# A chunked recurrence with an FFN on one core: other streams of constants on TensorE ahead of chunks 0 and 1

## The chip, the cores and the metric

One core of one Trainium2 chip. The metric is the device time of one execution in microseconds (us), as the median over runs. A smaller number is better. The engines are named as in the profile: PE is TensorE (PEld its weight loads), DVE is VectorE, ACT is ScalarE, POOL is GpSimd, and SP is the engine that issues most of the DMAs.

## The reference

First a recurrence with a state per head (batch 4, 8 heads, 768 steps, head size 48), then a feed-forward network over its output (3072 tokens, 384 wide, 2048 hidden), all in float32:

```python
for t in range(S):
    kt, vt, rt, wt = (k[:, :, t], v[:, :, t], r[:, :, t], w[:, :, t])
    cur = np.einsum('bhd,bhe->bhde', u[None] * kt, vt)
    y[:, :, t] = np.einsum('bhd,bhde->bhe', rt, state + cur)
    state = wt[:, :, :, None] * state + np.einsum('bhd,bhe->bhde', kt, vt)
...
h = x @ w_in
g = h * (1.0 / (1.0 + np.exp(-1.702 * h)))
return (g @ w_out).astype(np.float32)
```

## The kernel before, in words

**Tiling.** The recurrence is cut into 24 chunks of 128 steps (6 for each batch, numbered t = 0 to 23). A chunk has all 8 heads in 4 pairs. For one chunk, `chunk(t)` does these steps, in this order, with a `yield` between them:

- two running products of the decay on DVE (L352, L357), and the scaled k and r, `kq`, on DVE (L363);
- four transposes of the scaled k on PE into `ps_t` (L373), copied to `kt` by ACT (L375);
- the product r*k, `rku`, on DVE (L384), and the diagonal products `ps_d` on PE (L396), copied to `s` by ACT (L399), from which ACT makes the diagonal blocks `am` (L406, 8 instructions);
- the state products (L427) and the products of k and r (L431) on PE into `ps_u`;
- the new state on DVE (L437 to L441; the first chunk of a batch copies on ACT, L435), and the masked blocks put into `am` on DVE (L444);
- the output products on PE into `ps_y`: those with `am` (L454), the first half of those with the state (L467, `inter(True)`), then a copy of one element by ACT into `mid` (L477), which the second half (`inter(False)`, L467 again) has to wait for, then the copy out (L491, or L279 and L280).

A third generator, `measures` (token m), has ACT square and sum a chunk's running products (L285). The feed-forward network is done in tasks of one block of 128 hidden units by up to 512 tokens: first product (g, L526 plain or L531 to L533 split), gelu (h) and second product (y, L566 or L569 to L571). Weights are fetched (f) and converted (w) on ACT and DVE (L261 to L275) in the first 100 us or so.

**What sets the order.** The program is scheduled by hand. The string `RAMP` is a list of tokens, each of which issues one step: `a3` is the next step of chunk 3, `l2` the next loads of chunk 2, `m1` the measure of chunk 1, `g0`, `h0`, `y0` the steps of task 0. Each engine runs its own instructions in the order in which they were issued. After RAMP, rules set the order.

**The streams of constants.** A token `d6` does not issue work by itself. It puts (6, 4) on the list `cold`; the next call of `bank`, which hands out a PSUM bank, takes it off and issues six matmuls of a constant tile `warm` (128x128 in bfloat16, all ones, set by DVE in L124) with itself, 512 columns each, into the bank that was just handed out (L313). What they write is overwritten by the products that the bank was taken for.

```python
while cold:
    times, n = cold.pop()
    for _ in range(times):
        T.matmul(x.rearrange("p (n c) -> p n c", c=P)[:, 0:n], warm, warm_b[:, 0:n], start=True, stop=True)
```

In the kernel before, `d20` stands at the start (ahead of chunk 0's transposes), `d6` ahead of chunk 1's transposes, and after them `d5`, `d3`, `d7` and `d2` in other places. In the trace all of them have line L313.

Of the kernel before, what the change touches and what calls it, by code (L numbers as in the profile page):

```python
# [9 lines left out]
F32 = mybir.dt.float32  # L10
F32R = mybir.dt.float32r
BF16 = mybir.dt.bfloat16
# [10 lines left out]
P = 128  # L23
# [3 lines left out]
R2 = HB + D  # L27
# [55 lines left out]
AHEAD = (1, 1, 2, 2)  # L83
FIRST = 37
RAMP = """
d20 l0 l0 l1 a0 a0 a0 M m0 a0 a0 a1 a1 l0 a0 a0 a0 f0 a1 d6 l2 a0 a1 a1 a1 l1 l2 m1 a0 l3 a1 a1 a2 a2 a1 a1 a0 a0 d5
a2 w0 a3 a0 d3 a1 a2 d7 a1 a2 f1 a3 a3 a2 l3 a1 f2 x1 w1 a2 a2 a3 l4 a3 a3 a3 w0 a2 a2 d2 m2 f3 d2 a3 g0 w1 a3 h0 a3
a2 w2 w2 g1 h1 a2 y0 a2 a3 a4 w3 l4 g2 f4 a3 w3 h2 a3 w1 a4 w0 y1 w2 g3 y2 w0 h3 g4 w3 h4 m3 a4 w2 w4 y3 y4 f5 x3 s0
w1 a4 a4 g5 g6 w4 h5 w3 s0 w5 g7 h6 f6 w5 l5 g8 y5 w4 h7 a4 l6 f7 w4 a4 l5 h8 a4 a5 g9 y6 f8 h9 a5 w5 g10 y7 w5 w6 y8
y9 a5 h10 g11 w7 m4 a5 w6 f9 y10 a4 a5 a4 w6 h11 w8 w7 w6 g12 w7 a4 w8 a5 y11 g13 w7 a5 f11 h12 g14 y12 a6 h13 f10 a6  # L90
w9 y13 w9 l7 h14 w8 a5 w11 w8 a5 a4 m5 g15 a6 y14 w10 a5 a7 w9 a6 w10 g16 a6 h15 w9 h16 w11 g17 l8 w10 a6 a6 w10 y15
w11 w11 y16 g18 h17 a4 l6 a7 h18 u a5 a6 a5 l7 a7 m6 a6 a6 a8 g19 a7 a7 a5 a8 h19 y17 a6 m7 a7 a7 l8 a6 a7 a7 a8 a7 a6
l9 y18 a8 a8 a8 a9 l10 a7 l9 a8 a8 a7 a7 g20 a9 y19 x7 h20 a9 a8 a8 m8 y20 l10 a10 g21 a9 a9 h21 a10 l11 g22 a9 y21
h22 a9 a8 a9 a8 a9 m9 a9 a10 a11 y22 g23 a10 a10 a10 g24 a8 h23 a9 l11 a10 a11 a10 a9 a11 h24 a10 y23 m10 a11 a11 y24
a11 a9 g25 a11 l12 a10 a11 a11 a11 l13 h25 a10 a11 a10 a10 a12 a12 m11 a12 a11 a13 a11 a12 y25 l12 g26 l14 g27 g28 h26
g29 y26 g30 h27 g31 a13 y27 h28 a12 m12 h29 h30 g32 y28 g33 h31 a13 a13 y29 y30 y31 h32 g34 h33 h34 g35 y32 g36 h35
y33 h36 y34
"""
WIDE = 512
GAP = 64  # L100
# [8 lines left out]
def rwkv_ffn_kernel(ctx: ExitStack, tc, wkr, vp, vrk, ub, w_in, w_out, masks, vt, uc, out):  # L109
# [10 lines left out]
    at = fast.enter_context(tc.tile_pool(name="at", bufs=1))  # L120


    warm = at.tile([P, P], BF16, name="warm")
    V.memset(warm, 1.0)  # L124
    hm = cp.tile([R2, 2 + 2 * H], F32, name="hm")
    G.memset(hm, 0.0)
# [38 lines left out]


    A.activation(at.tile([R2, 1], F32, tag="s", name="junk", bufs=2), hm[:, 0:1], AF.Gelu_apprx_sigmoid)
    warm_b = warm.unsqueeze(1).broadcast_to([P, WIDE // P, P])

    his, los, whole = {}, {}, {}  # L170

# [133 lines left out]
    def bank(name):  # L305

        i = free.pop(0)
        x = ps_a.tile([P, WIDE], F32, tag=f"bank{i}", name=name)
        held[id(x)] = i, x
        while cold:  # L310
            times, n = cold.pop()
            for _ in range(times):
                T.matmul(x.rearrange("p (n c) -> p n c", c=P)[:, 0:n], warm, warm_b[:, 0:n], start=True, stop=True)  # L313
        return x

    def release(*xs):
# [290 lines left out]
    with tc.manual_schedule():  # L607
        early = ExitStack()
        su = early.enter_context(tc.tile_pool(name="su", bufs=1))
        where = [(i, col) for i, n in enumerate(CHUNKS) for col in range(n)]  # L610
        starts = [sum(CHUNKS[:i]) for i in range(len(CHUNKS))]
        last = {}
        for j, task in enumerate(TASKS):
            last[task[0]] = j
        running, told = {}, {}

        def piece(kind, i):

            if (kind, i) not in running:
                running[kind, i] = {  # L620
                    "l": load, "a": chunk, "m": measures.get, "w": lambda i: convert(i, su, False),
                    "s": lambda i: split_x(),
                }[kind](i)
            next(running[kind, i])

        def do(token):
            kind, i = token[0], int(token[1:] or 0)
            told[token] = told.get(token, 0) + 1
            if kind in "lamws":
                piece(kind, i)  # L630
                if kind == "w" and all(told.get(f"w{n}") == 4 for n in range(2 * NL)):
                    early.close()
                    pools["late"] = fast.enter_context(tc.tile_pool(name="late", bufs=2))

                    pools["late"].tile([P, GAP], F32, tag="gap", name="gap", bufs=1)
                    xs[1] = new_x(1)
            elif kind == "f":
                fetch(i, su)
            elif kind == "x":
                group, col = where[i]  # L640
                if i == 1:
                    fill_x(xw[0].unsqueeze(1) if WHOLES else xs[group], 0, 2 * C)
                elif i == 3:
                    fill_x(xs[group], 2 * C, 4 * C)
                elif group and col == CHUNKS[group] - 1:
                    fill_x(xs[group], 0, (col + 1) * C)
            elif kind in "de":
                cold.append((i, WIDE // P if kind == "d" else 2))
            elif kind == "u":
                pools["u"] = pools["late"].tile([P, DM], F32, tag="u", name="u_sb", bufs=1)  # L650
                nc.sync.dma_start(pools["u"], ub)
            elif kind == "M":
                nc.sync.dma_start(hm[ROWS, 0 : 2 + H], masks)
            elif kind == "g":
                first_product(i, TASKS[i])
            elif kind == "h":
                gelu(i, TASKS[i])
            elif kind == "y":
                group = TASKS[i][0]
                if i in (len(TASKS) - 9, len(TASKS) - 4):  # L660
                    next(judged)
                if i == len(TASKS) - 1:
                    bad.append(nc.values_load(cnt, min_val=0, max_val=full) < full)
                    finish(i)
                elif i < len(TASKS) - 3:
                    second_product(i, TASKS[i])
                if i == last[group] and i < len(TASKS) - 1:
                    store(group, starts[group] * C, CHUNKS[group] * C)

        def judge():  # L670

            sums = acc[:, NT : 3 * NT]
            V.tensor_tensor(sums, sums, sums, op=ALU.mult)
            for x, limit in ((acc[:, 0 : 3 * NT], LIMIT), (acc[:, 3 * NT :], W_MAX)):
                V.tensor_single_scalar(x, x, limit, op=ALU.is_lt)
            oks = at.tile([P, 1], F32, tag="s", name="oks", bufs=2)
            V.tensor_reduce(oks, acc, axis=AX.X, op=ALU.add)
            yield  # L680
            got = bank("ps_n")
            ps = got[0:1, 0:1]
            T.matmul(ps, oks, oks, start=True, stop=True)
            V.tensor_copy(cnt, ps)
            release(got)
            yield

        cnt = acc[0:1, 0:1].bitcast(I32)
        full = P * acc.shape[1] ** 2
        bad, judged = [], judge()  # L690

        def rest():

            begins = []
            for t, (i, col) in enumerate(where):
                n = len([x for x in TASKS if x[0] == i - 1])
                begins.append(last.get(i - 1, -1) + 1 - BEFORE - round((CHUNKS[i] - 1 - col) * n / CHUNKS[i]))
            left = []
            for t, begin in enumerate(begins):
                ramp = dict(told)  # L700
                for k, (kind, step, half, rank) in enumerate(PARTS):
                    token = f"{kind}{t + 2 * (kind == 'l')}"
                    if t in BY_BLOCKS and k < len(AHEAD):
                        step -= AHEAD[k] + (k == 3 and where[t][1] == 2)
                    elif t + 2 in BY_BLOCKS and kind == "l" and step == 3:
                        step -= 2
                    if kind == "l" and t + 2 >= NT:
                        continue
                    if ramp.get(token, 0):
                        ramp[token] -= 1  # L710
                    else:
                        left.append((step + begin, half, rank, token))
            left.sort(key=lambda x: x[:3])
            for j in range(FIRST, len(TASKS) + LAG):
                for post in range(3):
                    if post and j < len(TASKS):
                        yield f"{'gh'[post - 1]}{j}"
                    while left and left[0][:2] <= (j, post):
                        yield left.pop(0)[3]
                if j - LAG >= 0 and f"y{j - LAG}" not in told:  # L720
                    yield f"y{j - LAG}"

        for token in RAMP.split():
            do(token)
        for token in rest():
            do(token)
# [119 lines left out]
```

## Time and profile before

| | |
|---|---|
| median of 3 runs | 494.29 us (493.68 to 495.75) |
| the profiled execution | 494.09 us |
| its span, first to last instruction | 492.4 us |
| PE busy | 482.0 us (98%) |
| DVE busy | 298.9 us (61%) |
| ACT busy | 227.1 us (46%) |
| mean granted TensorE clock | 0.997 of full speed |
| DMA moved | 51.60 MB, mean 105 GB/s |

The profiled execution took 1.7 us more than its span, which lies around the first and the last instruction. A busy PE is not a PE at its peak: the end of a matmul is modelled, and a small matmul counts some 0.2 us from start to end however few columns it has. The granted clock is told as a share of full speed, where 1.00 is 2.4 GHz and 0.50 is 1.2 GHz.

### The profile page before, as it was taken

What the parts mean: (1) busy time and instruction counts of PE and PEld (TensorE: products, weight loads), DVE (VectorE), ACT (ScalarE), POOL (GpSimd) and SP (SyncE); (2) the same over time, 40 slices, a digit from 0 to 9 for tenths busy, and PEclk for the clock granted to TensorE, in tenths of its full rate; (3) what the DMA queues carried; (4) which work ended last, traced back from release to release, by engine and by line L of the source; (5) the groups of instructions that cost most, each with busy time, mean ns of one, the idle gap of its engine ahead of it and who ended that gap; (6) DMA issues with size and microseconds to landing.
All of it is one profiled execution on the core that took longest, in us unless ns stands there. A gap on an engine that the chain in (4) does not pass through costs nothing.

```text
span 492.4 us, 11658 instructions
## 1 busy us (share of the span) xinstructions
PE 482.0 (98%) x4891; PEld 395.0 (80%) x4891; DVE 298.9 (61%) x508; ACT 227.1 (46%) x518; POOL 15.9 (3%) x49
## 2 busy tenths in 40 slices
PE   7999999999999999999999999999999999999996
PEld 3678988887877887888888878888888878888885
DVE  8989999989888333855755745745845421111211
ACT  3799999865354332533433532342542332322221
POOL 3011000001001000000001000001000000000000
PEclk9899999999999999999999999999999999999999
DMA  8986949155721425062243252243340001100002
GB/s 220 260 242 193 276 128 237 48 148 157 208 57 34 124 88 117 23 185 81 81 119 98 75 173 71 81 140 85 92 154 20 4 1 32 64 1 0 1 0 73
DMA packets 34254, 51.60 MB, mean 105 GB/s; under 512 B 4336, under 2 KB 24240, under 8 KB 34192
## 3 DMA queue, kind: packets, MB, share of 16 engines
q1 hardware_dynamic: 33152, 48.84, 34.0%
q0 software_dynamic: 784, 1.39, 1.3%
q8 instruction: 40, 0.66, 0.6%
q10 hardware_dynamic: 256, 0.52, 0.3%
q14 instruction: 22, 0.18, 0.1%
HBM read 40.88 MB, written 7.60 MB: 98 GB/s over the span
## 4 chain that ended last, share of the span: by engine, by line
PE 84%; DVE 5%; DMA 4%; ACT 2%; issue 2%; SPq 1%; POOL 1%; DVEq 0%; ACTq 0%; POOLq 0%
PE ph L531 12%; PE po L569 12%; PE ph L533 11%; PE ph L532 11%; PE po L571 11%; PE po L570 11%; PE ps_y L467 3%; PE ps_y L454 2%; PE ps_u L431 2%; PE ps_u L427 2%; DMA far<-kb 2%; DMA kx<-far 2%; PE ph L526 1%; PE po L566 1%; PE po L595 1%
## 5 line engine op out<-in xcount | busy, mean ns | idle before, releaser
L551 DVE TENSOR_TENSOR gl<-gf,gh 128x512 fp32r<-128x512 f32 (+1 forms) x96 | 64.6, 673 | 145.5 <-ACT gf L549 144.8
L548 ACT ACTIVATE gh<-ph 128x512 fp32r<-128x512 f32 (+1 forms) x96 | 56.3, 586 | 185.5 <-PE ph L533 173.2
L531 PE MATMUL ph<-x,h 128*128 128x512 f32 (+1 forms) x288 | 111.5, 387 | 0.1
L533 PE MATMUL ph<-x,l 128*128 128x512 f32 (+1 forms) x288 | 110.6, 384 | 0.0
L532 PE MATMUL ph<-x,h 128*128 128x512 f32 (+1 forms) x288 | 110.5, 384 | 0.0
L569 PE MATMUL po<-gh,h 128*128 128x512 f32 (+1 forms) x279 | 109.5, 392 | 0.0
L571 PE MATMUL po<-gl,h 128*128 128x512 f32 (+1 forms) x279 | 107.3, 385 | 0.0
L570 PE MATMUL po<-gh,l 128*128 128x512 f32 (+1 forms) x279 | 107.2, 384 | 0.0
L531 PEld LDWEIGHTS ph<-x,h 128*128 128x128 f32 x288 | 54.1, 188 | 11.2 <-DMA x<-x 0.5
L533 PEld LDWEIGHTS ph<-x,l 128*128 128x128 f32 x288 | 54.1, 188 | 10.8
L532 PEld LDWEIGHTS ph<-x,h 128*128 128x128 f32 x288 | 54.2, 188 | 10.4
L571 PEld LDWEIGHTS po<-gl,h 128*128 128x128 f32 x279 | 52.5, 188 | 10.9 <-DVE gl L551 0.4
L569 PEld LDWEIGHTS po<-gh,h 128*128 128x128 f32 x279 | 52.4, 188 | 10.7
L570 PEld LDWEIGHTS po<-gh,l 128*128 128x128 f32 x279 | 52.5, 188 | 9.7
L549 ACT ACTIVATE gf<-ph 128x512 f32<-128x512 f32 (+1 forms) x96 | 56.0, 583 | 4.7 <-DVE gl L551 4.6
L363 DVE TENSOR_TENSOR kq<-wkr_t,lp 112x1024 f32<-112x1024 f32 x24 | 29.3, 1222 | 1.1 <-PE ps_y L467 0.6
L352 DVE TENSOR_TENSOR_SCAN lp<-wkr_t,d1r 112x516 f32<-112x516 f32 x24 | 29.4, 1224 | 0.9 <-POOL same L154 0.9
L357 DVE TENSOR_TENSOR_SCAN lp<-wkr_t,d1f 112x516 f32<-112x516 f32 x24 | 29.4, 1225 | 0.1
L285 ACT ACTIVATE junk<-lp 112x1032 bf16<-112x1032 f32 x24 | 25.5, 1065 | 5.2 <-DVE lp L357 5.2
L467 PE MATMUL ps_y<-kq,mid 48*48 48x64 f32 (+3 forms) x384 | 23.1, 218 | 1.4 <-ACT mid L477 1.1
L510 POOL DMA_DIRECT2D x<-x x18 | 9.0, 507 | 371.1 <-DVE x L280 199.0
L467 PEld LDWEIGHTS ps_y<-kq,mid 48*48 48x48 f32 (+3 forms) x384 | 18.7, 127 | 2.7 <-ACT mid L477 1.2
(107 smaller groups left out, 511.9 us busy)
## 6 DMA issues: line engine op xcount, KB each, us to landing
st<-in_w_out SPq DMA_DIRECT2D x6, 1024.0 KB
rk_t<-in_vrk SPq DMA_DIRECT2D x16, 384.0 KB
st<-in_w_in SPq DMA_DIRECT2D x6, 896.0 KB
v_t<-in_vrk SPq DMA_DIRECT2D x24, 192.0 KB
out_t<-ob SPq DMA_DIRECT2D x15, 256.0 KB
wkr_t<-in_wkr SPq DMA_DIRECT2D x18, 192.0 KB
wkr_t<-in_wkr SPq DMA_DIRECT2D x36, 96.0 KB
wkr_t<-in_wkr SPq DMA_DIRECT2D x5, 577.9 KB
```

The lines of the kernel that those rows point to most:

```text
L352: V.tensor_tensor_scan(li[:, ::-1], w1[:, ::-1], d1r.rearrange("r p c -> r (p c)")[:, ::-1], 0.0, op0=ALU.mult, op1=ALU.add)
L357: V.tensor_tensor_scan(pm, w0, d1f.rearrange("r p c -> r (p c)"), 0.0, op0=ALU.mult, op1=ALU.add)
L467: T.matmul(ps[b][head(h), p], from_[head(half), p * D + OFF * h : p * D + HB], qf[head(half), p, blocks[b]], start=False, stop=p == PAIRS[ ...
L531: T.matmul(ph, h_, xs[i][:, 0, c, cs], start=c == 0, stop=False)
L532: T.matmul(ph, h_, xs[i][:, 1, c, cs], start=False, stop=False)
L533: T.matmul(ph, l_, xs[i][:, 0, c, cs], start=False, stop=c == NM - 1)
L548: A.activation(gh, ph, AF.Gelu_apprx_sigmoid, scale=1.0 / W_SCALE)
L549: A.activation(gf, ph, AF.Gelu_apprx_sigmoid, scale=1.0 / W_SCALE)
L551: V.tensor_tensor(gl, gf, gh.bitcast(F32), op=ALU.subtract)
L569: T.matmul(o, h_, gh, start=first, stop=False, skip_group_check=True)
L570: T.matmul(o, l_, gh, start=False, stop=False, skip_group_check=True)
L571: T.matmul(o, h_, gl, start=False, stop=f == NF - 1, skip_group_check=True)
```

## The change

The constant tile becomes 128x112 in float32. A second view of it, `lights`, reads its first 64 columns as 128 columns of bfloat16 (so that ones and zeros alternate). The old tokens d use `lights`. A new token c issues float32 matmuls: 112x112 weights, 4 times 112 columns. The list `cold` is now emptied in the order in which it was filled. In RAMP, `d20` becomes `c5 d7`, `d6` becomes `d7`, and two tokens `d1` are new: one ahead of chunk 1's diagonal products and one ahead of its state products. A float32 matmul leaves two records in the trace (as the `ps_d` products do, 4 matmuls and 8 records), so that the 20 + 6 records of before stand against 10 + 7 + 7 + 1 + 1 = 26 records of the change.

```diff
 RAMP = """
-d20 l0 l0 l1 a0 a0 a0 M m0 a0 a0 a1 a1 l0 a0 a0 a0 f0 a1 d6 l2 a0 a1 a1 a1 l1 l2 m1 a0 l3 a1 a1 a2 a2 a1 a1 a0 a0 d5
...
+c5 d7 l0 l0 l1 a0 a0 a0 M m0 a0 a0 a1 a1 l0 a0 a0 a0 f0 a1 d7 l2 a0 a1 a1 d1 a1 l1 l2 m1 a0 l3 a1 d1 a1 a2 a2 a1 a1 a0
...
-    warm = at.tile([P, P], BF16, name="warm")
+    warm = at.tile([P, R2], F32, name="warm")
     V.memset(warm, 1.0)
...
-    warm_b = warm.unsqueeze(1).broadcast_to([P, WIDE // P, P])
+    lights = warm.bitcast(BF16)[:, 0:P]
+    warms = [x.unsqueeze(1).broadcast_to([P, WIDE // P, x.shape[1]]) for x in (warm, lights)]
...
         while cold:
             times, n = cold.pop()
             for _ in range(times):
-                T.matmul(x.rearrange("p (n c) -> p n c", c=P)[:, 0:n], warm, warm_b[:, 0:n], start=True, stop=True)
+                w = warms[n > 0]
+                m, k = w.shape[2], n or WIDE // P
+                T.matmul(x.rearrange("p (n c) -> p n c", c=P)[0:m, 0:k, 0:m], w[:, 0], w[:, 0:k], start=True, stop=True)
...
-            elif kind in "de":
-                cold.append((i, WIDE // P if kind == "d" else 2))
+            elif kind in "cde":
+                cold.insert(0, (i, {"c": 0, "d": WIDE // P, "e": 2}[kind]))
```

The rest of RAMP holds the same tokens in the same order. On DVE only the size of the constant's memset differs, and on ACT, POOL and SP nothing does.

**The first place** is the start of PE's order, up to chunk 0's transposes (`ps_t<-ident,kq`). Before, it ends with the last of twenty pairs of a weight load and a matmul:

```order
L313 LDWEIGHTS warm
L313 MATMUL ps_t<-warm 128x512
L373 MATMUL ps_t<-ident,kq_89 128x112 x4
L396 MATMUL ps_d<-hm,rku 128x2 x4
L427 MATMUL ps_u_194<-v_t_86,kt 64x48
```

With the change, where every line after the head of the file stands three lower (L316 for L313), five float32 matmuls and seven pairs stand there, of which the first is shown:

```order
L844 UNCONDITIONAL_BRANCH
L316 MATMUL ps_t<-warm 112x4x112 x5
L316 LDWEIGHTS warm
L316 MATMUL ps_t<-warm 128x512
...
L376 MATMUL ps_t<-ident,kq_89 128x112 x4
L399 MATMUL ps_d<-hm,rku 128x2 x4
```

Nothing else moved there: the transposes, the diagonal products and the state products of chunk 0 follow without a stream between them, as before.

**The second place** is chunk 1 on PE, from the last product of chunk 0's `ps_u` to chunk 1's first state product. Before (the first of six pairs is shown):

```order
L431 MATMUL ps_u_195<-kq_89 64x64
L313 LDWEIGHTS warm
L313 MATMUL ps_t<-warm 128x512
...
L373 MATMUL ps_t<-ident,kq_90 128x112 x4
L396 MATMUL ps_d<-hm,rku 128x2 x4
L427 MATMUL ps_u_274<-v_t_87,kt 64x48
```

With the change (the first of seven pairs is shown):

```order
L434 MATMUL ps_u_187<-kq_89 64x64
L316 LDWEIGHTS warm
L316 MATMUL ps_t<-warm 128x512
...
L376 MATMUL ps_t<-ident,kq_90 128x112 x4
L316 LDWEIGHTS warm
L316 MATMUL ps_d<-warm 128x512
L399 MATMUL ps_d<-hm,rku 128x2 x4
L316 LDWEIGHTS warm
L316 MATMUL ps_u_268<-warm 128x512
L430 MATMUL ps_u_268<-v_t_87,kt 64x48
```

One pair is added ahead of the transposes, one between them and the diagonal products, and one between these and the state products.

## Rows read from the trace of the kernel before

**Rows 1.** The page: busy time by engine; then PE's granted clock in 40 slices.

```profile
PE 482.0 (98%) x4891; PEld 395.0 (80%) x4891; DVE 298.9 (61%) x508; ACT 227.1 (46%) x518; POOL 15.9 (3%) x49
...
PEclk9899999999999999999999999999999999999999
```

**Rows 2.** Stretches: window, length, busy PE, PEld, DVE, ACT, POOL, granted clock, DMA.

```profile
7.52:9.29 1.77, 0.00 (x0) 0.03 (x1) 1.74 (x3) 1.16 (x2) 0.00 (x0) 1.00 1.03 271
9.29:11.82 2.53, 2.53 (x76) 2.35 (x76) 2.46 (x4) 1.37 (x5) 0.00 (x0) 1.00 1.04 223
11.82:15.24 3.42, 3.42 (x19) 1.78 (x12) 3.39 (x7) 1.55 (x7) 0.00 (x0) 0.50 0.86 244
15.24:19.79 4.55, 3.46 (x122) 3.23 (x121) 4.13 (x8) 4.36 (x14) 0.00 (x0) 1.00 0.84 225
```

**Rows 3.** The chain that ended last, 9 to 23 us: start, length, what.

```profile
9.16 0.14 issue
...
11.94 2.67 PE ps_t L313 x6
...
15.40 0.53 ACT kt L375
15.93 1.05 ACT junk L285 x2
16.98 0.06 ACT s L399
...
19.09 0.05 ACT mid L477
...
19.85 1.83 PE ps_y L313 x8
...
22.77 0.53 PE ps_t L373 x4
```

**Rows 4.** PE in order of time: start, length, what, count, [idle before].

```profile
1.14 6.38 PE L313 MATMUL ps_t<-warm 128*128 128x512 bf16 x20 [1.14 <-DVE warm L124]
9.29 0.57 PE L373 MATMUL ps_t<-ident,kq 112*128 112x112 f32 x4 [1.77 <-DVE kq L363]
...
14.41 0.95 PE L373 MATMUL ps_t<-ident,kq 112*128 112x112 f32 x4
...
19.18 0.67 PE L467 MATMUL ps_y<-kq,mid 64*64 64x64 f32 x8 [1.09 <-ACT mid L477]
```

**Rows 5.** A later stretch, columns as in rows 2.

```profile
20.00:25.00 5.00, 5.00 (x82) 3.10 (x81) 4.86 (x6) 3.75 (x14) 0.00 (x0) 1.00 1.03 292
```

**Rows 6.** Weight loads of the first stream in order of time.

```profile
4.53 0.15 PEld L313 LDWEIGHTS <-warm 128*128 128x128 bf16 x1 [0.28 <-issue]
4.96 2.06 PEld L313 LDWEIGHTS <-warm 128*128 128x128 bf16 x10 [0.28 <-issue]
```

**Rows 7.** The chain at 42 us: six records of float32 products, 256 columns.

```profile
42.83 1.29 PE po L566 x6
```

**Rows 8.** DVE in order of time, chunk 1's `kq` and what follows.

```profile
12.41 1.23 DVE L363 TENSOR_TENSOR kq<-wkr_t,lp 112x1024 f32<-112x1024 f32 x1
...
18.88 0.77 DVE L444 COPY_PREDICATED am<-after,ps_u 128x256 f32<-128x256 int32 x2
19.89 1.23 DVE L363 TENSOR_TENSOR kq<-wkr_t,lp 112x1024 f32<-112x1024 f32 x1 [0.24 <-PE ps_y L467]
...
26.35 0.69 DVE L384 TENSOR_TENSOR rku<-wkr_t 112x512 f32<-112x512 f32 x1 [0.82 <-PE ps_d L396]
```

**Rows 9.** ACT in order of time, chunk 0's diagonal products read.

```profile
10.89 0.17 ACT L399 COPY s<-ps_d 128x8 f32<-128x8 f32 x1 [0.46 <-PE ps_d L396]
```

**Rows 10.** In order of time: a weight fetch (SP), its first reader (ACT), row copies (POOL).

```profile
14.91 1.35 SPq L243 DMA_DIRECT2D st<-in_w_out  x1
...
24.69 1.14 ACT L261 ACTIVATE st<-st 128x1024 int32<-128x1024 uint32 x1
...
25.10 1.60 POOL L510 DMA_DIRECT2D l<-l  x3 [19.93 <-ACT l L491]
```

More of the change, by code (lines that the diff above doesn't have):

```diff
@@ L85 @@
 RAMP = """
-d20 l0 l0 l1 a0 a0 a0 M m0 a0 a0 a1 a1 l0 a0 a0 a0 f0 a1 d6 l2 a0 a1 a1 a1 l1 l2 m1 a0 l3 a1 a1 a2 a2 a1 a1 a0 a0 d5
[L87 to L95, printed above, removed]
@@ L96 @@
-g29 y26 g30 h27 g31 a13 y27 h28 a12 m12 h29 h30 g32 y28 g33 h31 a13 a13 y29 y30 y31 h32 g34 h33 h34 g35 y32 g36 h35
-y33 h36 y34
+c5 d7 l0 l0 l1 a0 a0 a0 M m0 a0 a0 a1 a1 l0 a0 a0 a0 f0 a1 d7 l2 a0 a1 a1 d1 a1 l1 l2 m1 a0 l3 a1 d1 a1 a2 a2 a1 a1 a0
+a0 d5 a2 w0 a3 a0 d3 a1 a2 d7 a1 a2 f1 a3 a3 a2 l3 a1 f2 x1 w1 a2 a2 a3 l4 a3 a3 a3 w0 a2 a2 d2 m2 f3 d2 a3 g0 w1 a3
+h0 a3 a2 w2 w2 g1 h1 a2 y0 a2 a3 a4 w3 l4 g2 f4 a3 w3 h2 a3 w1 a4 w0 y1 w2 g3 y2 w0 h3 g4 w3 h4 m3 a4 w2 w4 y3 y4 f5
+x3 s0 w1 a4 a4 g5 g6 w4 h5 w3 s0 w5 g7 h6 f6 w5 l5 g8 y5 w4 h7 a4 l6 f7 w4 a4 l5 h8 a4 a5 g9 y6 f8 h9 a5 w5 g10 y7 w5
@@ new lines @@
+w6 y8 y9 a5 h10 g11 w7 m4 a5 w6 f9 y10 a4 a5 a4 w6 h11 w8 w7 w6 g12 w7 a4 w8 a5 y11 g13 w7 a5 f11 h12 g14 y12 a6 h13
+f10 a6 w9 y13 w9 l7 h14 w8 a5 w11 w8 a5 a4 m5 g15 a6 y14 w10 a5 a7 w9 a6 w10 g16 a6 h15 w9 h16 w11 g17 l8 w10 a6 a6
+w10 y15 w11 w11 y16 g18 h17 a4 l6 a7 h18 u a5 a6 a5 l7 a7 m6 a6 a6 a8 g19 a7 a7 a5 a8 h19 y17 a6 m7 a7 a7 l8 a6 a7 a7
+a8 a7 a6 l9 y18 a8 a8 a8 a9 l10 a7 l9 a8 a8 a7 a7 g20 a9 y19 x7 h20 a9 a8 a8 m8 y20 l10 a10 g21 a9 a9 h21 a10 l11 g22
+a9 y21 h22 a9 a8 a9 a8 a9 m9 a9 a10 a11 y22 g23 a10 a10 a10 g24 a8 h23 a9 l11 a10 a11 a10 a9 a11 h24 a10 y23 m10 a11
@@ L98 @@
+a11 y24 a11 a9 g25 a11 l12 a10 a11 a11 a11 l13 h25 a10 a11 a10 a10 a12 a12 m11 a12 a11 a13 a11 a12 y25 l12 g26 l14 g27
+g28 h26 g29 y26 g30 h27 g31 a13 y27 h28 a12 m12 h29 h30 g32 y28 g33 h31 a13 a13 y29 y30 y31 h32 g34 h33 h34 g35 y32
+g36 h35 y33 h36 y34
 """
```

## The prediction

> **What bounds the kernel now.** I read the page first [rows 1]: PE is busy 98% of the span, and its granted clock is clearly below full in one slice alone, the second (12 to 25 us). So PE sets the time, and what the change can win or lose lies in the first 25 us. The busy time by stretches [rows 2] shows the place: PE idle from 7.52 to 9.29 us, small products until 11.82 at a granted 1.00, then 3.42 us at 0.50 (1.2 GHz), and 1.00 again (2.4 GHz) from 15.24 us.
>
> The chain of waits [rows 3] tells whether this costs time. It runs through the six constant matmuls ahead of chunk 1's transposes (2.67 us), through these transposes at the lower clock, then through ACT (the copy of `kt`, the measure L285, `s`, the eight `am`, the copy into `mid`), and back to PE at 19.18 us for the second half of chunk 0's output products. PE had waited 1.09 us for that copy [rows 4]. From 20 us on it has no idle time in the next stretch [rows 5]. So what chunk 1's transposes gain or lose comes out at 19.18 us, and moves a PE that hardly rests afterwards.
>
> **Durations.** In the first stream the weight loads, one for each matmul, are 0.43 us apart until 4.96 us (4.53 to 4.96), and then ten of them take 2.06 us, 0.21 apart [rows 6]. For 512 columns that is the pace of 1.2 GHz and then of 2.4 GHz, although the granted clock stands at 1.00 from the start. So in this execution the clock rose near 5.0 us, 3.8 us after the stream's start at 1.14 [rows 4]. The trace has no float32 matmul of 448 columns. The nearest row is six float32 records of 256 columns in 1.29 us, 0.215 each [rows 7]; by columns that makes 0.215 x 448/256 = 0.376 us for one record at full clock (estimate), and 0.75 at half.
>
> **The change part by part.**
>
> *`c5 d7` for `d20`.* Ten float32 records and seven bfloat16 ones stand against twenty. With the clock rising at 4.96 us as before, five records at 0.75 from 1.2 us end at 4.95, five at 0.376 end at 6.83, and seven at 0.215 end at 8.33 us. Before, the stream ended at 1.14 + 6.38 = 7.52. Chunk 0's transposes wait for DVE's `kq` and start at 9.29 either way [rows 4], so the direct cost is nothing, and PE's idle time ahead of them falls from 1.77 to 0.96 us. If the rise came one microsecond later, the end would move by about half of that (each record started at half clock costs 0.37 more, and one starts every 0.75); the cover is gone where the rise comes after some 6.6 us.
>
> *`d7` for `d6`, and the clock there.* This decides the sum. If the clock stays at full, seven matmuls take 7 x 0.215 = 1.5 us from 11.94, until 13.44. Then chunk 1's transposes wait for their `kq`, which DVE ends at 12.41 + 1.23 = 13.64 [rows 8]. With the 0.14 us that lay between the two for chunk 0 [rows 3] they start at 13.78, take chunk 0's 0.57 instead of 0.95 [rows 4], and end at 14.35. They ended at 14.41 + 0.95 = 15.36. That is 1.01 us.
>
> *The two `d1`.* 0.215 us each, on PE. From the end of chunk 1's transposes to the wait at 19.18 - 1.09 = 18.09, PE's products took 2.73 us; with both `d1` they end at 14.35 + 2.73 + 0.43 = 17.51. ACT, 1.01 earlier, reaches the `mid` copy at 18.08, so PE still waits for ACT, by half a microsecond. The diagonal products ended 0.99 us after chunk 0's transposes (ACT took them at 10.89, after a wait [rows 9]); with one `d1` that is 15.6 for chunk 1, and ACT wants them at 16.98 - 1.01 = 15.97. Both `d1` are covered; without that cover they would cost 0.43.
>
> *The memset, the order of `cold`, the bits of `lights`.* Nothing: the tile is 448 bytes per partition against 256, on a DVE that soon waits for POOL; only `c5` and `d7` are ever on the list together; and the columns are as many.
>
> *Does the microsecond live on?* The second half of chunk 0's output products starts at 18.17 instead of 19.18. DVE's next `kq` waited only 0.24 us for it [rows 8], because DVE is busy with `am` until 19.65. It comes 0.24 earlier, then, and ends at 20.88, while PE, 1.01 earlier, wants it for chunk 2's transposes at 21.76 (22.77 in [rows 3]): no wait. Further on DVE waits 0.82 us for PE's `ps_d` at 26.35 [rows 8], and there it gains what it lacked. Two things need not move with PE: the weight fetch issued at 14.91 and read at 24.69, and the copies of rows issued at 25.10 [rows 10]. The read shows no wait, and the copies are issued by what PE and ACT finish, so I let both move. If the fetch lands only just in time today, nothing of the gain is left: the lower end, 0. The upper end is 1.01, because DVE's `kq` forbids more. I take **0.95**, near the upper end, as no row shows a wait on that way.
>
> *Is the clock held?* Here I chose. Chunk 0: 4.42 us without a stream (7.52 to 11.94), of it 1.77 idle, and the clock fell at 11.82 [rows 2]. Chunk 1: from the end of its stream (11.94 + 2.67 = 14.61) to the next at 19.85 there are 5.24 us without one, of it 1.09 idle, and the clock stayed at 1.00 [rows 2 to 4]. The changed kernel has 3.6 us without a stream (8.33 to 11.94), of it 0.96 idle: less of both than the stretch that held. By the nearer row the clock holds.
>
> **Sum.** Against the profiled execution's own time: 494.09 - 0.95 = 493.1. The median of the runs stands 0.2 above that execution, so the forecast is **493.3 us**. That is 0.2%; about 0.5% (2.5 us) is what a measurement of this kernel can tell from no change.
>
> **The rivals.**
>
> *The clock falls all the same.* For it: chunk 0's own products from 9.29 to 11.82 are unchanged, and they are the last that PE does before the fall. Against it: the same kinds of product kept 1.00 after chunk 1's stream. Then `d7` is one matmul more at half clock, 0.43 us, ahead of the transposes; as these then lie further into the time after the rise at 15.24, they end 0.25 to 0.43 later, and the two `d1` stay under ACT. Result 494.3 + 0.35 = 494.6 us. The Trainium skill bears on this case ("TensorE: Matmul & The Clock Gate", section "Why this matters for your kernels"): it lets the clock drop after long idle gaps between bursts of matmuls, longer ones than any in this stretch. By that rule a gap of 1.77 us was not what lowered the clock, a shorter one would not keep it up, and the time would be this rival's. The trace agrees only in part: the clock did fall after so short a gap, so something less than the page asks for is enough.
>
> *The gain is lost at a transfer.* The clock holds, but the fetch or the row copies [rows 10] end the wait instead of PE. Against it: no wait is on record there. Result 494.1 to 494.3 us.
>
> *The first stream runs over.* Slower. If float32 records did not lift the clock at all, ten at 0.75 and seven at 0.43 would end at 11.7 us. Chunk 0's transposes would start 2.4 us late and take 0.38 longer, DVE's state step would wait for what follows them, and the seven at half clock behind them would take 3.0 us for the six's 2.67. In all 3.1 us, 497.4 us. It decides from a rise later than 6.6 us. Against it: float32 records keep PE streaming without a pause, as the bfloat16 ones did. The skill's same page ("What you observe") has the rise vary by half a microsecond from run to run. By that the stream would end at 8.1 to 8.6 us, still ahead of 9.29, and this rival would not come in.
>
> *The change does more than the stretch shows.* Since the rest is ordered by hand, a shift of 1 us could free a later wait. Of PE's idle time, 492.4 - 482.0 = 10.4 us, 4.0 lie before 19.2 [rows 1, 4] and 6.4 after it, the end of the program included. A third of these would give 491.2 us.
>
> **How the numbers follow.** Clock held and gain kept: 0.53. Clock falls: 0.26. Lost at a transfer: 0.11. First stream over: 0.06. More than the stretch shows: 0.04. Faster by over 0.5% (below 491.8) has 0.04, slower by over 0.5% (above 496.8) 0.06, within it 0.90. The range takes the first three cases: from 493.3 less 0.7, about what the lowest run of before lies under its median, which is 492.6, to the second case plus 0.5 of scatter, 495.1. The first case's own range is 492.6 to 494.0.
>
> **What would show it.** Right: a granted clock of 1.00 from 11 to 16 us; seven constant matmuls in about 1.5 us ahead of chunk 1's transposes; these waiting for `kq` and taking about 0.57; ACT's `kt` copy near 14.4; the second half of chunk 0's output products at about 18.2; the end about 1 us earlier. Wrong: 0.50 in that stretch; a first stream that ends after 9.2 us; a new wait of PE between 20 and 32 us, on a DMA or on ACT.

## The result, and the profile after

The changed kernel takes 497.16 us (median of 22 runs, 495.15 to 501.17); the kernel before takes 493.9 us (22 runs, 492.47 to 497.62). The ratio is 1.007 with a 95% interval of 1.005 to 1.0091: slower by 0.7%, where 0.2% faster was forecast. Ratios here and below leave out the one execution (503.32 us, of `count_back`) that lay over 1.5% above the fastest of its kernel. The profiled execution took 496.89 us with a span of 495.2 us, against 494.09 and 492.4.

The first 20 us went as forecast. The chain that ended last, 12 to 21 us, changed kernel (start, length, what), to be held against [rows 3]:

```profile
12.59 1.24 DVE kq L366
13.83 0.04 issue
13.87 0.62 PE ps_t L376 x4
14.49 0.02 issue
14.51 0.53 ACT kt L378
15.04 1.05 ACT junk L286 x2
...
18.11 0.14 ACT mid L480
18.25 0.04 issue
18.30 0.68 PE ps_y L470 x8
```

Chunk 1's transposes wait for `kq` and no longer for the stream, the copy of `kt` starts at 14.51 (forecast near 14.4), and the second half of chunk 0's output products at 18.30 (forecast 18.17), 0.88 us earlier than before. The granted clock stayed at 1.00 where it had been 0.50 in [rows 2] (stretches of the changed kernel, columns as there):

```profile
12.00:16.00 4.00, 3.82 (x33) 2.08 (x25) 3.89 (x7) 3.05 (x11) 0.00 (x0) 1.00 0.98 232
```

So the mechanism worked in this execution, and 3.6 us were lost behind it: from 0.88 ahead at 18 us to 2.7 behind at 481 us. The page has them as busy time of PE, 482.0 before [rows 1] and 486.6 now, not as waiting (1.9 of these 4.6 us are the longer first stream, which fills time that was idle):

```profile
PE 486.6 (98%) x4891; PEld 395.5 (80%) x4891; DVE 298.9 (60%) x508; ACT 227.6 (46%) x518; POOL 15.9 (3%) x49
...
PEclk9999999999999999999999999999999999999999
```

With a full clock and as many instructions, PE was busy for longer. I paired each PE instruction with its counterpart in the other trace and followed the difference of their starts. It steps at two or three places, but most of it grows steadily in three stretches, about 157 to 190, 280 to 342 and 424 to 481 us. Two stretches by windows show it; PE is without idle time in both. Before:

```profile
360.00:400.00 40.00, 40.00 (x398) 33.17 (x397) 19.45 (x39) 14.64 (x32) 0.00 (x0) 1.00 0.14 48
430.00:480.00 50.00, 50.00 (x222) 41.11 (x221) 9.44 (x18) 13.04 (x24) 0.00 (x0) 1.00 0.00 1
```

After:

```profile
360.00:400.00 40.00, 40.00 (x398) 33.14 (x397) 19.17 (x39) 13.81 (x31) 0.00 (x0) 1.00 0.15 49
430.00:480.00 50.00, 50.00 (x218) 40.40 (x216) 8.95 (x16) 13.06 (x24) 0.00 (x0) 1.00 0.02 6
```

From 360 to 400 us the same 398 matmuls run; from 430 to 480 us only 218 instead of 222. PE in order of time shows which are slower. Before, a row of first products (L531 to L533) and the second product behind them:

```profile
439.98 0.39 PE L531 MATMUL ph<-x,h 128*128 128x512 f32 x1
440.21 0.39 PE L532 MATMUL ph<-x,h 128*128 128x512 f32 x1
440.44 0.39 PE L533 MATMUL ph<-x,l 128*128 128x512 f32 x1
440.66 0.39 PE L569 MATMUL po<-gh,h 128*128 128x512 f32 x1
```

After:

```profile
441.93 0.39 PE L534 MATMUL ph<-x,h 128*128 128x512 f32 x1
442.17 0.39 PE L535 MATMUL ph<-x,h 128*128 128x512 f32 x1
442.40 0.39 PE L536 MATMUL ph<-x,l 128*128 128x512 f32 x1
442.63 0.39 PE L572 MATMUL po<-gh,h 128*128 128x512 f32 x1
442.86 0.40 PE L573 MATMUL po<-gh,l 128*128 128x512 f32 x1
443.10 0.39 PE L574 MATMUL po<-gl,h 128*128 128x512 f32 x1
443.32 0.40 PE L572 MATMUL po<-gh,h 128*128 128x512 f32 x1
```

Three first products take 0.68 us before and 0.70 after. Averaged over a token group's 144 of them (start to start, from the trace): 226.7 to 226.9 ns in all groups from 2 on before; after, 233.3 ns in groups 1, 3 and 5 and still 226.9 and 226.7 in groups 2 and 4.

The odd groups have one thing in common: their `x` lies in the pool `late`, that of the even groups in `mo` (`new_x`, L190). The constant tile grew from 256 to 448 bytes per partition, and pools are stacked, so all that lies behind it is 192 bytes higher: in the built programs `x` of the odd groups starts at byte 198944 before and 199136 after. The weights and the `x` of the even groups lie ahead of that tile and did not move. Modulo 256 the weights and both `x` started at 32 before; now the odd groups' `x` starts at 224.

The theory (A): the distance of the moving operand to the weights costs 6.6 ns per matmul, that is 3 groups x 144 x 6.6 = 2.85 us, and about 0.5 more in the odd groups' second products (0.5 to 1.7 ns each on 144 apiece). The second products' own operands had not moved. In group 5 a row has nine second products. From the second to the fifth, the next matmul starts 236, 228, 233 and 231 ns later; from the others 226 or 227 ns, as before. So a slow row reaches a few matmuls into the row behind it; why is not shown.

The rival (B): the new streams shift something later that costs the time.

### The profile page after: what moved, and what is told of

It reads as the page before. It is cut to its first block, busy times and chain, and to the rows that moved or that the text cites. A ratio compares the mean times of both kernels' runs of the same rounds, so it can differ in the third digit from the quotient of the medians.

```text
span 495.2 us, 11657 instructions
## 1 busy us (share of the span) xinstructions
PE 486.6 (98%) x4891; PEld 395.5 (80%) x4891; DVE 298.9 (60%) x508; ACT 227.6 (46%) x518; POOL 15.9 (3%) x49
## 4 chain that ended last, share of the span: by engine, by line
PE 91%; DVE 3%; DMA 2%; ACT 1%; issue 1%; SPq 0%; DVEq 0%
PE ph L534 13%; PE po L572 13%; PE ph L535 13%; PE ph L536 13%; PE po L573 12%; PE po L574 12%; PE ps_y L470 3%; PE ps_y L457 3%; PE ps_u L434 2%; PE ps_u L430 2%; PE ph L529 1%; PE po L569 1%; PE po L598 1%; PE ps_d L399 1%; PE ps_t L376 1%; DMA kx<-far 1%
## 5 line engine op out<-in xcount | busy, mean ns | idle before, releaser
L534 PEld LDWEIGHTS ph<-x,h 128*128 128x128 f32 x288 | 54.1, 188 | 11.5
```

Of the source, the lines that this page charges most:

```text
L534: T.matmul(ph, h_, xs[i][:, 0, c, cs], start=c == 0, stop=False)
```

## The experiments

Paces are means between the starts of successive 512-column matmuls, over one group. Ratios are to the kernel before in the same job; its median differs by job and chip, 493.9 to 496.1 us.

### The address and the streams, apart

`e1_gap16`: the changed kernel with `x` of the odd groups put back.

```diff
-GAP = 64
+GAP = 16
```

> The changed kernel with the filler tile ahead of x in the pool late cut from 64 to 16 columns (256 to 64 bytes), so that x of the odd groups lies again where it lay before; streams and all else as changed. Theory A (the 192 bytes by which the larger constant tile moves x cost the time): the first-product matmuls of groups 1, 3 and 5 come every 226.7 ns again instead of 233.3, and the streams' gain of 0.9 us at 18 us is kept: 0.9 us faster than before, 493.0 against 493.9, 4 us faster than the changed kernel. Theory B (the new streams cost the time, by what they shift later): as the changed kernel, ratio to before near 1.007, 497.

Measured: 226.7 ns in groups 3 to 5 (227.3 in group 1), and 223 instructions from 430 to 480 us. Ratio 0.9993 (0.9959 to 1.0026). The address part of theory A held; the 0.9 us of the streams did not show, see below.

```profile
430.00:480.00 50.00, 50.00 (x223) 41.14 (x222) 9.70 (x18) 13.28 (x25) 0.00 (x0) 1.00 0.00 1
```

`e2_shift_late`: the kernel before with only that pool moved.

```diff
-GAP = 64
+GAP = 112
```

> The kernel before, with its old streams, and the filler tile in the pool late raised from 64 to 112 columns: x of the odd groups, rk and ob lie 192 bytes higher, nothing else differs. Theory A: 233.3 ns for each first-product matmul of groups 1, 3 and 5, that is 432 x 6.6 ns = 2.9 us, and a few tenths more in the second products: 3 to 4 us slower than before, ratio 1.006 to 1.008. Theory B: no difference from before.

Measured: 233.3 ns in groups 1, 3 and 5, 226.9 and 226.7 in groups 2 and 4, with the old streams. Ratio 1.0051 (1.002 to 1.0081), about 2.5 us. B falls: a change of one filler, with no stream touched, makes most of the loss.

`e3_shift_all`: the kernel before with the constant tile as large as after.

```diff
-    warm = at.tile([P, P], BF16, name="warm")
+    warm = at.tile([P, 2 * R2], BF16, name="warm")[:, 0:P]
```

> The kernel before, with its old streams, but the constant tile allocated at 448 bytes per partition of which the first 256 are used: every address as in the changed kernel. Theory A: like the shift of the pool late alone, 3 to 4 us slower than before; if it is slower than that one by over 0.5 us, tiles of the pool at (kq, lp, kt, am) have a part of their own. Theory B: no difference from before.

Measured: the same paces, 233.3 in the odd groups. Ratio 1.0031 (0.9995 to 1.0067), not to be told from `e2_shift_late`, nor by its time alone from no change: no part of the other moved tiles shows.

`e4_shift_everything`: the kernel before with nearly everything 192 bytes higher, the weights too.

```diff
-FILL = 44
+FILL = 92
```

> The kernel before, with the filler at the end of the constants' pool raised from 44 to 92 columns: all tiles after it, weights, x of all groups, gelu outputs and the rest, lie 192 bytes higher, so x keeps its distance to the weights. Theory A1 (the address of x by itself decides): all first-product matmuls, those of the even groups too, take 233.3 ns, 864 x 6.6 = 5.7 us slower at least, and the second products may follow. Theory A2 (the distance of x to the weights, modulo some power of two, decides): 226.7 ns everywhere, no difference from before. Theory B: no difference.

Measured: 226.7 ns in groups 3 to 5, 227.6 and 226.9 in groups 1 and 2, 223 instructions from 430 to 480 us. Ratio 0.9979 (0.9949 to 1.0008). The odd groups' `x` is here at the very byte, 199136, at which it was slow. So not the address decides but the distance to what moved along, A2. PE in both kinds of stretch, first `e2_shift_late`:

```profile
360.00:400.00 40.00, 40.00 (x398) 33.17 (x397) 18.82 (x38) 14.46 (x32) 0.00 (x0) 1.00 0.15 49
430.00:480.00 50.00, 50.00 (x218) 40.30 (x217) 8.95 (x16) 13.15 (x25) 0.00 (x0) 1.00 0.01 2
```

then `e4_shift_everything`:

```profile
360.00:400.00 40.00, 40.00 (x398) 33.17 (x397) 19.44 (x39) 13.57 (x30) 0.00 (x0) 1.00 0.15 49
430.00:480.00 50.00, 50.00 (x223) 41.13 (x222) 8.95 (x16) 13.65 (x26) 0.00 (x0) 1.00 0.02 7
```

### The picture turned round

`mo_up`: 192 bytes ahead of `x` in the pool `mo`, taken out again in `late`, old streams.

```diff
     mo = ctx.enter_context(tc.tile_pool(name="mo", bufs=2))
+    mo.tile([P, 48], F32, tag="up", name="up", bufs=1)
...
-GAP = 64
+GAP = 16
```

> The kernel before, with 192 bytes put ahead of x in the pool mo and taken out of the filler in the pool late: x of the even groups and the gelu outputs gh and gl of all groups lie 192 bytes higher against the weights, x of the odd groups lies where it lay. If the distance to the weights decides: the picture turned round, 233.3 ns for the first products of the even groups (387 matmuls in groups 0, 2 and 4), 226.7 in the odd ones, and the second products of all groups near 233 as well (some 800 matmuls): (387 + 800) x 6.6 ns = 7.8 us slower than before, ratio near 1.016. If it were only the place of the odd groups' x: no difference from before.

Measured: ratio 1.0138 (1.0095 to 1.0181), about 6.8 us slower. First products 233.6 and 233.4 ns in the even groups, 228.7 to 229.4 in the odd ones; second products, whose moving operands `gh` and `gl` are in `mo`, 233.2 to 233.8 in all groups. PE from 360 to 400 us, in an even group, now has 394 instructions instead of 398:

```profile
360.00:400.00 40.00, 40.00 (x394) 32.42 (x393) 22.53 (x44) 16.23 (x35) 0.00 (x0) 1.00 0.17 56
430.00:480.00 50.00, 50.00 (x219) 40.52 (x218) 8.95 (x16) 14.71 (x28) 0.00 (x0) 1.00 0.04 16
```

The loss follows the distance into whichever products have it, the second products too. The odd groups' first products were forecast at 226.7 ns; here again it is the matmuls just behind a slow row that lose, although their own operands have not moved. Since `x` of the even groups and `gh` and `gl` moved together, what counts is the distance to the weights and not the one to each other.

### Which distances

The kernel before with only the filler of `late` changed, four times, one profile each: `GAP` 72, 80, 96 and 48.

> The kernel before with the filler of the pool late at 72 columns: x of the odd groups 32 bytes higher than before, weights where they were. With 192 bytes the odd groups' first products came every 233.3 ns instead of 226.7. If the distance modulo 256 or 128 decides, 32 is a new value: either pace, 226.7 if only whole steps of 64 count, since two streams that lie within one step of 64 would meet alike.

> As before, x of the odd groups 64 bytes higher. If the distance modulo 128 decides, 64 is the same as 192: 233.3 ns in groups 1, 3 and 5. If modulo 256, it is a value of its own and may be either.

> As before, x of the odd groups 128 bytes higher. If the distance modulo 128 decides, this is no shift at all: 226.7 ns. If modulo 256, it is half way round and the farthest from the old distance: 233.3 ns or more.

> As before, x of the odd groups 64 bytes lower, which is the same as 192 bytes higher modulo 256, 128 and 64, but another address. If a modulus decides: 233.3 ns in groups 1, 3 and 5. If something else of the 192 bytes decides (where the tile ends, what it comes to lie over): 226.7 ns.

| `x` against before | first products, odd groups | second products, group 5 |
|---|---|---|
| 0 | 226.7 ns | 227.0 ns |
| 32 bytes up | 233.4 | 230.4 |
| 64 bytes up | 229.2 to 229.5 | 231.2 |
| 128 bytes up | 232.7 to 232.8 | 229.1 |
| 192 bytes up | 233.3 | 228.7 |
| 64 bytes down | 233.3 | 228.7 |

64 down and 192 up agree to the tenth, so this goes by the distance modulo 256. Modulo 128 is ruled out: 128 up is slow, and 64 up differs from 192 up. Modulo 512 is ruled out by the kernel before, where `x` of the even groups starts at byte 120864 and that of the odd ones at 198944, which are 256 apart modulo 512, and both are equally fast. The guess that only whole steps of 64 count was a miss. Of the six rows, only distance 0 is fast; at 64 up the first products lose least and the second products behind them most. Each of the four took 495.98 to 498.04 us beside 492.14 for the kernel before, single executions.

### What the streams are worth

With the address in order, the streams should have given 0.9 us. `e1_gap16` was run again:

> The changed streams with x of the odd groups back in its old place, once more, for the streams' own worth. If the clock holds ahead of chunk 1's transposes in every execution and the 0.9 us are kept: ratio 0.998. If it holds only in some, or the microsecond is lost to the weight fetch as in the first profile: 0.999 to 1.0005, not to be told from before.

Measured: 0.9994 (0.9962 to 1.0026). Two things took the gain, and the profiles show both. A third is that in some executions the kernel with the old streams has the clock at 1.00 there too.

In `e1_again` the clock fell all the same (stretches, columns as in [rows 2]):

```profile
10.90:14.30 3.40, 3.40 (x69) 2.36 (x69) 3.30 (x6) 2.39 (x10) 0.00 (x0) 0.50 0.98 222
```

The pace of its first stream doubled near 4.0 us, in the changed kernel's profile near 6.7. The profile in which it doubled later held the clock, the other did not. But `count_back` (below) held it after a doubling near 4.2 us, so with the new first stream this alone does not decide.

In the first profile of `e1_gap16` the clock held and the second half of chunk 0's output products came 1.03 us earlier; by 31 us PE was 0.40 us behind the kernel before. ACT in order of time shows the first loss:

```profile
24.64 1.18 ACT L262 ACTIVATE st<-st 128x1024 int32<-128x1024 uint32 x1 [0.87 <-DMA st<-in_w_out]
```

The chain of the same profile, 22 to 33 us, shows the second:

```profile
22.93 0.85 ACT l L494 x4
23.78 0.30 issue
24.08 6.71 DMA l<-l
30.78 0.25 issue
31.03 1.58 PE ph L529 x6
```

The weight fetch read at 24.69 before [rows 10] came in at 24.64, however early ACT was there, and the copies of rows took 6.7 us. These are the two transfers that I had let move with PE.

The third: with the old first stream, too, the clock does not always fall where [rows 2] has it. Twelve profiles have a first stream of old matmuls alone. In six of them the pace doubled at 3.8 to 5.2 us, and the clock was at 0.50 over the stream ahead of chunk 1's transposes, which started at 14.3 to 15.3 us. In the other six it doubled at 5.7 to 6.2 us, these transposes started at 13.6 to 14.0 us at a granted 1.00, as with the new streams, and the clock fell near 16 us. `e4_shift_everything` is one of these:

```profile
12.00:15.00 3.00, 2.30 (x15) 1.15 (x13) 2.96 (x6) 2.05 (x9) 0.00 (x0) 1.00 0.93 242
16.50:19.00 2.50, 2.26 (x64) 2.05 (x56) 2.26 (x6) 1.88 (x9) 0.00 (x0) 0.50 0.99 267
```

By 22 us its PE was 1.8 us behind that of the kernel before's profile. So the 0.88 us are a gain over one kind of execution only.

Every execution of the experiments has a mean granted clock on record. In their three jobs the kernel before took 493.9 to 494.5 us (medians) where that was 0.994 or more (53 of 93 executions) and 495.6 to 496.9 us where it was less, some 2 us more. The changed streams, with `x` in either place, had 0.994 or more in 41 of 46. So they may well hold the clock up more often; but at 0.994 or more `e1_gap16` and `e1_again` took 494.8 and 494.3 us, the kernel before beside them 494.5 and 494.3. At that clock `e2_shift_late` is 3.1 us slower than before and `mo_up` 7.7, near the 3.3 and 7.6 us by which their matmuls lie further apart in the profiles. This division was made after the runs and tested by none.

Then the two halves of the change, both with `x` in its old place:

```diff
-c5 d7 l0 l0 l1
+d20 l0 l0 l1
```

> As the one before, but the first stream is the old twenty bfloat16 matmuls; the streams at chunk 1 (seven, one, one) are the new ones. If what holds the clock is the longer first stream, which ends later: the first stream ends near 7.5 to 8 us, the clock falls to 0.50 between 10 and 16 us as in all profiles with the old streams, and the time is 0.3 us above before. If the streams at chunk 1 hold it: 1.00 throughout.

Measured: 0.9977 (0.9953 to 1.0002); in its one profile the clock was 0.50 from 11.5 to 14.9 us. The forecast of a loss was a miss, and the profile had nothing of a gain that the clock could have made. Nor had the clock fallen ahead of chunk 1 in all profiles with the old streams, as it took for given: of the eight there were by then, four had it fall near 16 us, behind chunk 1's transposes.

```diff
-a1 d7 l2 a0 a1 a1 d1 a1 l1 l2 m1 a0 l3 a1 d1 a1 a2
+a1 d6 l2 a0 a1 a1 a1 l1 l2 m1 a0 l3 a1 a1 a2
```

> As the second, but the streams at chunk 1 are the old six; the first stream is the new one (five float32, seven bfloat16). If the longer first stream holds the clock: 1.00 through chunk 1, its transposes near 13.8 and the time that of the whole change with x in its old place. If both parts are needed: a fall to 0.50 somewhere from 11 to 20 us.

Measured: 1.0046 (1.0021 to 1.0072), which neither theory gives. PE's waits by releaser, 240 to 360 us, have more of one kind, for `kt`, which comes by way of two DMAs. Before, then here:

```profile
PE ps_u L427 <- ACT kt L380: 1.1, 1, 1.1
PE ps_u L430 <- ACT kt L383: 2.8, 3, 1.3
```

This kernel has 23 records in these two streams, three fewer than the kernel before and the changed one (26; `streams_chunk1_only` has 29). Three runs tested whether that number decides.

`count_back`: `c5 d10` at the start, old streams at chunk 1, 26 records.

> The first stream new (five float32 matmuls, then ten bfloat16 ones instead of seven), chunk 1's streams old, x of the odd groups in its old place: the kernel that came out 0.46% slower, with three more constant matmuls, so that PE has as many records as before (26 in these two streams). If the number of PE's records ahead of the rest decides (by where later instruction fetches and transfers fall): as before, ratio 0.998 to 1.001. If the new first stream itself costs the time: 1.0045 again, and 0.3 us more.

Measured: 0.9991 (0.9971 to 1.0012). Its profile has the clock at 1.00 throughout, 0.82 us gained at 18 us, and again lost to transfers by 31 us.

`count_minus_3`: the kernel before with `d17` for `d20`.

> The kernel before with seventeen matmuls in the first stream instead of twenty, nothing else: three records fewer, the same number as in the slow kernel. If the number of records decides: slower, ratio near 1.0045, by longer waits of PE for the copies of kt between 240 and 360 us. If not: 0.999 to 1.001.

Measured: 1.003 (1.0001 to 1.0058); five of its twelve runs lie at 493.1 to 495.1 us and seven at 496.6 to 498.9. Six of the seven have a mean granted clock of 0.984 to 0.993, the five 0.994 to 1.000. The one profile, with a span of 492.0 us, doesn't show the longer waits that were expected.

`count_plus_3`: `d23` for `d20`.

> The kernel before with twenty-three matmuls in the first stream, nothing else: three records more, the same number as in the kernel with the new streams at chunk 1 only (ratio 0.9977). If the number of records made that one fast: 0.998. If its streams did: 0.999 to 1.001.

Measured: 0.9996 (0.9974 to 1.0018). More records don't make the kernel faster.

So both kernels with three records fewer came out slower, by 1.5 and 2.3 us, and the one that has them back did not. That the number is the cause is not shown: the interval of `count_minus_3` barely leaves out no change, and at a granted clock of 0.994 or more it took 494.3 us against 493.9 before. `streams_start_only` is slower there too, 497.0 against 494.3. Each has one profile, and that of `count_minus_3` doesn't show where the time goes. The changed kernel has 26 records, so this is no part of its loss.

## Why the prediction was wrong

**The step that failed** is the part on the constant tile, priced at nothing: "The memset, the order of `cold`, the bits of `lights`. Nothing: the tile is 448 bytes per partition against 256, on a DVE that soon waits for POOL". I priced the larger tile as a memset. It is also 192 bytes that move every later tile, and with `x` of the odd groups off its distance to the weights, 432 matmuls take 6.6 ns more each (2.85 us; against the paces of before, group by group, 2.7) and the second products of these groups about 0.5 us. `e2_shift_late` has that loss without the change, `e1_gap16` has the change without that loss, and `mo_up` moves it to the first products of the even groups and to all second products.

**Sum of the changed profile**: 0.88 gained at 18.30, 3.2 lost by the distance (2.7 and 0.5, added up matmul by matmul against the trace of before), and a wait of 0.84 us at 113.9 for which the trace names only "issue"; together 3.2 behind, less 0.3 of the later wait for `kt`, which was shorter, makes 2.9; measured, 2.7 behind at 481 us. No other profile of these streams has that wait:

```profile
114.78 0.27 PE L434 MATMUL ps_u<-kq 48*64 48x64 f32 x1 [0.84 <-issue]
```

**`c5 d7` for `d20`.** The price of a record was right: weight loads start 0.75 us apart, then 0.37 (6.97 to 7.34):

```profile
5.74 0.31 PEld L316 LDWEIGHTS ps_t<-warm 128*112 128x112 f32 x1 [0.44 <-issue]
6.49 0.28 PEld L316 LDWEIGHTS ps_t<-warm 128*112 128x112 f32 x1 [0.44 <-issue]
6.97 0.18 PEld L316 LDWEIGHTS ps_t<-warm 128*112 128x112 f32 x1 [0.20 <-issue]
7.34 0.10 PEld L316 LDWEIGHTS <-warm 128*128 128x128 bf16 x1 [0.20 <-issue]
```

The clock's rise was later than in the profile of before, so the stream ended at 9.39 instead of 8.33 us, just past the edge that I had put at a rise after 6.6 us. By luck `kq` came 0.17 later there as well, so that chunk 0's transposes, at 9.47, started as soon after it as before.

**`d7` for `d6`, and the two `d1`.** Right in the profiled execution: 13.87 for 13.78, 18.30 for 18.17, and both `d1` under ACT (PE still waited 0.32 us for the `mid` copy).

**"Is the clock held?"** Right in three profiles with the new first stream (the changed kernel, `e1_gap16`, `count_back`), wrong in two (`e1_again`, `streams_start_only`). Two rows of one profile had decided it, and they didn't show how much the rise differs between executions: 3.8 to 6.7 us over all profiles. The Trainium skill ("TensorE: Matmul & The Clock Gate", "What you observe") gives half a microsecond either way; the traces here have some 1.5 either way. One of the two was also misread: of the 5.24 us without a stream that "held", the first 0.63 (14.61 to 15.24) still had 0.50 [rows 2], so the row shows a clock that had just risen, not one that held for 5.24 us.

**"Does the microsecond live on?"** It did to 100 us in the changed kernel, and not in the two other profiles that held the clock, where the weight fetch and the row copies ended the wait. So of the rivals two were at work, the clock that falls and the gain lost at a transfer, and together they leave nothing that 12 runs can tell: 0.9993 and 0.9994 for the streams alone. That slower came out has neither the place nor the cause of the rival that I had given 0.06.

## What to carry to other kernels

When a tile changes its size, compare the addresses of all tiles of the two programs before the durations: on a kernel that is bound by PE, a few ns per matmul can outweigh a wait at the start, as here. A loss that shows as busy time, with as many instructions and a full clock, is a change of pace; count instructions in stretches of equal length, group by group. And a gain of a microsecond taken from one profile is worth what is left of it in other executions, where the clock rises at another time and transfers land later.

## What the runs showed of the hardware

Back-to-back float32r matmuls of 512 columns, each with its own weights of 128x128, came every 226.7 ns where the moving operand started at the same place modulo 256 bytes as the weights, and every 229.2 to 233.4 ns at the other distances tried (32, 64, 128 and 192 bytes up; 64 down is 192 up); moving both left the pace at 226.7. Matmuls at distance 0 just behind such a row were slowed as well, to 228.7 to 231.2 ns in the mean of a group. The Trainium skill ("TensorE: Matmul & The Clock Gate", "Step-by-step: what each phase is for") has the weights of the next matmul load through a read port of their own, without taking bandwidth from the running one. By that one would not expect the distance to matter; here it costs up to 3%, and the measurement decides. What in the memory makes it was not tried.

No version was shown to beat the kernel before. The nearest is `streams_chunk1_only` at 0.9977 (0.9953 to 1.0002); the changed streams with `GAP = 16` undo the loss and no more.
